# Wider and fewer zeros products in the early gaps of TensorE, in an attention-and-MLP kernel

## The chip, the cores and the metric

The kernel runs on one core of one Trainium2 chip. The metric is the device time of one execution in microseconds, as the median of several runs. A profile of one execution goes with it: its span is the time from the first instruction of the program to the last.

## The reference

Eight batches of an approximate attention (8 heads, 576 tokens, head size 64, 32 landmarks) are followed by a two-layer MLP with a squared ReLU. Cut to what matters:

```python
q_lm = q.reshape(B, H, m, S // m, D).mean(axis=3)      # 32 landmark means, k_lm alike
A  = softmax(scale * q    @ k_lm.T)
Bm = softmax(scale * q_lm @ k_lm.T)
C  = softmax(scale * q_lm @ k.T)
Z  = Bm.T / (norm_1(Bm) * norm_inf(Bm) + 1e-6)
for _ in range(6):
    Z = 2 * Z - Z @ Bm @ Z
x = (A @ Z @ C @ v), heads side by side                 # 4608 x 512
h = x @ w_in                                            # 512 -> 2048
out = square(max(h, 0)) @ w_out                         # 2048 -> 512
```

## The kernel before

**Staging.** The program is written as a list of operations (`attention(b)`, `mlp_in(b)`, `mlp_out(b)` for eight batches b). Each operation names what it reads and writes and is a small function that issues one or more instructions. The order in which they are issued is not that of the list: the table `ORDER` (lines 34 to 149) holds it, worked out beforehand. A positive code is an operation, an engine for it and a PSUM bank. A negative code is a fill: `emit` (lines 205 to 215) takes the bank from the code's last three bits and the count from the rest. Every engine then runs its own instructions strictly in that order, and semaphores hold an instruction until its data is there.

**The fills.** A fill multiplies a tile of zeros by itself into a PSUM bank that no other operation uses at that point (lines 392 to 394). Nothing reads the result. There are 15 groups of them, all in the first 34 us, where TensorE has gaps: in issue order 77, 11, 7, 10, 1, 7, 24, 4, 6, 4, 3, 10, 8, 3 and 3 products, 178 in all. Each is one load of weights (LDWEIGHTS, 128x128) and one product of 128 columns. The first group of 77 stands before any other work of TensorE; the tile `zero` that it reads is cleared by VectorE in `constants3` (line 399), the first of that function's clearings.

**The early stretch.** GpSimd issues the loads: k and q of batch 0, v, then k and q of batch 1, the four pieces of w_in and of w_out. All of these go through one queue. TensorE runs, for batch 0: transposes of k and q (line 519), landmark means (436), their fold (449), the small landmark scores (544), the scores C (677) and A (779), transposes of C (700), the first Newton product (600) and its six steps (632), C times v (728), the matrix W (763), and the transposes of A (835). Between these stand the first steps of batch 1: its transposes (519), means (473), fold (490), and landmark scores (541). Then line 850 folds w_in into G, line 870 is the first MLP layer and line 934 the second; from about 34 us on, these two make up most of TensorE's work. A transpose of four heads (line 519) is one operation of 12 products that all read the same loaded tile `kqraw` and the constant `ident`.

**Evacuation.** ScalarE and VectorE copy results out of PSUM (lines 267, 269, 273, 275), take maxima, sums and exponentials; GpSimd multiplies masks and normalises A.

## Time and profile before

| | us |
|---|---|
| median of 3 runs (263.9 to 264.46) | 264.15 |
| the profiled execution, its own time | 262.73 |
| its span | 261.0 |
| TensorE busy with products in the span | 251.1 |
| VectorE, ScalarE, GpSimd busy | 183.7, 179.4, 83.5 |

How to read what follows: PE is TensorE's products and PEld its weight loads, which overlap the products; DVE is VectorE, ACT is ScalarE, POOL is GpSimd, SP the engine that issues the stores. L394 is line 394 of the kernel. In a list in order of time a row gives the start, the length, the engine, the line, the operation and what it writes and reads; in brackets stands how long the engine was idle before it and what ended the idle time. "Issue" means that nothing in the profile ended it. A product's length runs from its start to a modelled end, and products overlap, so what a product costs is the distance from one start to the next. In rows by stretch of time, `(x96)` counts the instructions that ran in it. The TensorE clock is given as the share of full speed that was granted. Queues are named q0, q1, q8 and q14; the page calls q8 and q14 "instruction".

### The profile page before, as it was taken

What the parts mean: (1) busy time and instruction counts of PE and PEld (TensorE: products, weight loads), DVE (VectorE), ACT (ScalarE), POOL (GpSimd) and SP (SyncE); (2) the same over time, 40 slices, a digit from 0 to 9 for tenths busy, and PEclk for the clock granted to TensorE, in tenths of its full rate; (3) what the DMA queues carried; (4) which work ended last, traced back from release to release, by engine and by line L of the source; (5) the groups of instructions that cost most, each with busy time, mean ns of one, the idle gap of its engine ahead of it and who ended that gap; (6) DMA issues with size and microseconds to landing.
All of it is one profiled execution on the core that took longest, in us unless ns stands there. A gap on an engine that the chain in (4) does not pass through costs nothing.

```text
span 261.0 us, 7449 instructions
## 1 busy us (share of the span) xinstructions
PE 251.1 (96%) x3040; PEld 153.8 (59%) x3040; DVE 183.7 (70%) x423; ACT 179.4 (69%) x357; POOL 83.5 (32%) x127
## 2 busy tenths in 40 slices
PE   8996999999999999999999999999999999999992
PEld 8984674665555566556655565456655555555551
DVE  2395686779859998798668977866997676664400
ACT  1376789979973799786976697688787576454221
POOL 6153823526133525312471239124513220000000
PEclk9999689999999999999999999999999999999998
DMA  6999999694999999999969998999994107000425
GB/s 81 201 202 207 204 183 204 103 183 77 216 194 195 169 195 231 189 188 173 197 126 207 199 198 179 203 163 194 186 75 101 52 0 186 23 23 1 141 63 141
DMA packets 73346, 39.48 MB, mean 151 GB/s; under 512 B 46048, under 2 KB 68832, under 8 KB 73312
## 3 DMA queue, kind: packets, MB, share of 16 engines
q0 software_dynamic: 23040, 18.35, 46.9%
q1 hardware_dynamic: 50272, 20.65, 41.0%
q8 instruction: 24, 0.39, 0.6%
q14 instruction: 10, 0.08, 0.1%
HBM read 36.70 MB, written 9.44 MB: 177 GB/s over the span
## 4 chain that ended last, share of the span: by engine, by line
PE 83%; DMA 9%; issue 3%; DVE 1%; POOL 1%; ACT 1%; POOLq 0%; ACTq 0%; DVEq 0%
PE ps L934 45%; PE ps L870 22%; DMA kqraw<-in_k_dram 5%; DMA kqraw<-in_q_dram 4%; PE ps L850 3%; PE ps L779 2%; PE ps L473 2%; PE ps L728 1%; PE ps L394 1%; PE ps L637 1%; PE ps L519 1%; PE ps L677 1%; PE ps L700 1%; PE ps L490 1%; PE ps L835 1%
## 5 line engine op out<-in xcount | busy, mean ns | idle before, releaser
L934 PE MATMUL ps<-w_out_bf,gs 128*128 128x512 bf16 (+1 forms) x592 | 148.8, 374 | 0.0
L934 PEld LDWEIGHTS <-gs 128*128 128x128 bf16 x592 | 53.9, 98 | 44.0 <-issue 5.2
L870 PE MATMUL ps<-AT,G 128*128 128x288 bf16 x512 | 79.4, 287 | 0.1
L886 ACT ACTIVATE r<-ps 128x576 bf16<-128x576 f32 x84 | 53.5, 652 | 20.3 <-PE ps L870 14.2
L870 PEld LDWEIGHTS <-G 128*128 128x128 bf16 x512 | 49.2, 98 | 25.2 <-ACT G L267 0.5
L576 POOL TENSOR_TENSOR Pd<-st,ones_d 128x256 bf16<-128x256 bf16 x42 | 28.7, 683 | 81.6 <-DVE st L648 59.4
L895 ACT ACTIVATE gs<-r 128x576 bf16<-128x576 bf16 x70 | 45.5, 680 | 6.9 <-DVE r L888 6.5
L888 DVE TENSOR_SCALAR r<-ps 128x576 bf16<-128x576 f32 x44 | 32.7, 750 | 14.5 <-PE ps L870 10.6
L267 ACT CAST G<-ps 128x512 bf16<-128x512 f32 x47 | 25.6, 588 | 7.5 <-PE ps L850 7.1
L897 DVE TENSOR_TENSOR gs<-r 128x576 bf16<-128x576 bf16 x58 | 27.6, 490 | 4.1 <-ACT r L886 3.5
L814 POOL TENSOR_TENSOR EA<-EA,rA 96x384 bf16<-96x384 bf16 x20 | 18.3, 926 | 10.6 <-DVE st L648 6.2
L267 ACT COPY o<-ps 128x512 f32<-128x512 f32 (+1 forms) x19 | 10.8, 575 | 15.6 <-PE ps L934 14.6
L648 DVE SCALAR_TENSOR_TENSOR st<-st,ps 128x128 bf16<-128x128 bf16 x40 | 11.3, 282 | 13.8 <-PE ps L637 7.4
L269 DVE COPY o<-ps 128x512 f32<-128x512 f32 (+1 forms) x18 | 12.1, 669 | 10.3 <-PE ps L934 10.3
L788 DVE TENSOR_REDUCE mxA<-ps 96x16 f32<-96x512 f32 x24 | 16.1, 679 | 3.6 <-ACT gs L895 1.7
L394 PE MATMUL ps<-zero 128*128 128x128 bf16 x178 | 16.0, 256 | 1.1 <-DVE zero L399 1.1
L791 DVE TENSOR_TENSOR SA<-ps,mxA 96x512 f32<-96x512 f32 x24 | 16.2, 680 | 0.3
L803 DVE TENSOR_REDUCE sA<-EA 96x24 f32<-96x768 bf16 x16 | 15.0, 940 | 0.4 <-ACT EA L797 0.3
L797 ACT ACTIVATE EA<-SA 96x512 bf16<-96x512 f32 x24 | 14.5, 626 | 0.7 <-DVE SA L791 0.7
L394 PEld LDWEIGHTS <-zero 128*128 128x128 bf16 x178 | 13.6, 118 | 1.3 <-DVE zero L399 1.1
L269 DVE CAST G<-ps 128x512 bf16<-128x512 f32 x17 | 11.4, 684 | 3.0 <-PE ps L850 2.9
L688 ACT ACTIVATE EC<-ps,nmc 128x576 bf16<-128x576 f32 x16 | 11.9, 743 | 2.2 <-DVE nmc L683 2.1
(109 smaller groups left out, 246.4 us busy)
## 6 DMA issues: line engine op xcount, KB each, us to landing
kqraw<-in_k_dram POOLq DMA_DIRECT2D x8, 576.0 KB, 7.2
kqraw<-in_q_dram POOLq DMA_DIRECT2D x8, 576.0 KB, 11.6
vraw<-in_v_dram POOLq DMA_DIRECT2D x8, 576.0 KB, 9.1
out_dram<-o SPq DMA_DIRECT2D x23, 192.0 KB, 2.6
out_dram<-o SPq DMA_DIRECT2D x24, 128.0 KB, 2.6
w_in_bf<-in_moe_w_in_dram POOLq DMA_DIRECT2D x4, 512.0 KB, 10.0
w_out_bf<-in_moe_w_out_dram POOLq DMA_DIRECT2D x4, 512.0 KB, 11.3
out_dram<-o SPq DMA_DIRECT2D x23, 64.0 KB, 2.1
```

Of the source, the lines that this page charges most:

```text
L267: nc.scalar.copy(dst, src)
L269: ENG[e].tensor_copy(dst, src)
L394: mm(ps[:, bank, 0:P], lhsT=zero[:], rhs=zero[:], start=True, stop=True)
L576: ENG[e].tensor_tensor(dst[:], src.unsqueeze(2).to_broadcast([P, 2, NG, M]), ones_d[:].unsqueeze(1).to_broadcast([P, 2, NG, M]), ALU.mult)
L791: add({"DVE": dve(512)}, lambda e, sa=sa, j=j: nc.vector.tensor_tensor(grouped(SA[:, j, :]), grouped(one(sa)[0:TP, :]), mxA[:, j, :].unsqu ...
L814: ENG[e].tensor_tensor(w, w, rA[:, i, cs, :].rearrange("p c g -> p (c g)").unsqueeze(2) .to_broadcast([TP, NJ * NG, M]), ALU.mult)
L870: mm(t[:, j, 0:HALF], lhsT=G[:, i, f * P:(f + 1) * P], rhs=AT[:, i, j * HALF:(j + 1) * HALF], start=(i == 0), stop=(i == 1))
L886: nc.scalar.activation(rj, src, AF.Relu)
L888: nc.vector.tensor_scalar(out=rj, in0=src, scalar1=0.0, scalar2=None, op0=ALU.max)
L895: nc.scalar.activation(dst, r[:], AF.Square)
L897: nc.vector.tensor_tensor(dst, r[:], r[:], ALU.mult)
L934: mm(one(ok)[:, 0:hi - lo], lhsT=gs[:, f, x0:x0 + P], rhs=w_out_bf[:, f, lo:hi], start=(f == f0), stop=(f == f1 - 1))
```

## The change

A fill becomes a loop over up to eight units of 64 columns at a time: products of 512 columns and one narrower product for what is left. The tile of zeros grows from 128 to 512 columns, and the first 128 of them are the weights. The 15 fill codes of `ORDER` are rewritten: the count now stands for units of 64 columns. The banks and the places in the order are the same, and no other code is changed.

```diff
-    136, 24, 64, 104, 176, -616, 880, 802, 928, 404, 448, 856, -93, 480, 528, -61, 962, 1040, 1016, 224, 608, 4344,
+    136, 24, 64, 104, 176, -1280, 880, 802, 928, 404, 448, 856, -197, 480, 528, -117, 962, 1040, 1016, 224, 608, 4344,
...
-    zero = sb.tile([P, P], BF16, name="zero")
+    zero = sb.tile([P, 512], BF16, name="zero")
 
     def fill(bank, n):
-        for _ in range(n):
-            mm(ps[:, bank, 0:P], lhsT=zero[:], rhs=zero[:], start=True, stop=True)
+        while n:
+            w = min(n, 8)
+            mm(ps[:, bank, 0:64 * w], lhsT=zero[:, 0:P], rhs=zero[:, 0:64 * w], start=True, stop=True)
+            n -= w
```

Group by group, in issue order (products before, units of 64 columns after, products after):

| before | units | after |
|---|---|---|
| 77 | 160 | 20 |
| 11 | 24 | 3 |
| 7 | 14 | 2 |
| 10 | 20 | 3 |
| 1 | 3 | 1 |
| 7 | 14 | 2 |
| 24 | 50 | 7 |
| 4 | 8 | 1 |
| 6 | 12 | 2 |
| 4 | 9 | 2 |
| 3 | 6 | 1 |
| 10 | 20 | 3 |
| 8 | 18 | 3 |
| 3 | 6 | 1 |
| 3 | 6 | 1 |
| 178 | 370 | 52 |

## The prediction

> **What bounds the kernel now.** I read the page's busy times and chain first, then TensorE's waits, then the first 36 us in order of time, because every edited product stands there.

> ```profile
> PE 251.1 (96%) x3040; PEld 153.8 (59%) x3040; DVE 183.7 (70%) x423; ACT 179.4 (69%) x357; POOL 83.5 (32%) x127
> ...
> PE 83%; DMA 9%; issue 3%; DVE 1%; POOL 1%; ACT 1%; POOLq 0%; ACTq 0%; DVEq 0%
> ...
> q8 instruction: 24, 0.39, 0.6%
> ```
> ```profile
> PE ps L519 <- issue: 2.5, 1, 2.5
> ...
> PE ps L519 <- DMA kqraw<-in_k_dram: 0.5, 1, 0.5
> PE ps L473 <- DMA kqraw<-in_q_dram: 0.4, 1, 0.4
> ```

> TensorE is the bound: 83% of the chain is its own work. After its start it stands still only three times for 0.4 us or more, and the longest, 2.5 us, is put down to "issue": no semaphore that the profile shows released it. The stretches behind the start (length, PE busy, count of products started or running, granted clock, DMA share, GB/s) say what a shift is worth:

> ```profile
> 34.36:62.00 27.64, 27.64 (x329) 1.00 0.91 152
> 62.00:77.00 15.00, 14.35 (x176) 1.00 1.16 182
> 77.00:250.00 173.00, 172.84 (x1891) 1.00 0.83 145
> ```

> From 34.36 to 250 us TensorE lacks 0.65 + 0.16 = 0.81 us of being always busy. A microsecond lost or won before 34 us therefore passes nearly whole to the end, and the question is only what the early part does.

> **The fills themselves.** 15 groups hold 178 products of 128 columns; after the change they hold 52 of up to 512. Columns go from 178 x 128 = 22784 to 370 units x 64 = 23680, 896 more.

> ```profile
> 1.06 7.14 PEld L394 LDWEIGHTS <-zero 128*128 128x128 bf16 x77 [1.06 <-DVE zero L399]
> ...
> 15.15 1.36 PEld L394 LDWEIGHTS <-zero 128*128 128x128 bf16 x24
> 17.13 0.54 PEld L519 LDWEIGHTS <-kqraw 96*128 96x128 bf16 x12 [0.62 <-DMA kqraw<-in_k_dram]
> ```
> ```profile
> 39.02 0.86 PE ps L934 x4
> ```

> Warm, a fill of 128 costs 1.36 / 24 = 57 ns, and a product of 512 columns (line 934) 0.86 / 4 = 215 ns. The group of 24 becomes six of 512 and one of 128: 6 x 215 + 57 = 1.35 us against 1.36. So width buys nothing in stream time; columns decide. The 77 products at the start took 7.14 us, 93 ns each, more than the warm 57, and I let columns decide there too: the first group has 10240 in place of 9856, 4% or at most 0.3 us more. The zero tile grows from 128 to 512 columns, and its clearing goes ahead of the first fill:

> ```profile
> 0.90 0.11 DVE L399 MEMSET zero<- 128x64 uint32 x1 [0.90 <-PEq L987]
> 1.01 0.27 DVE L400 MEMSET kbd<- 128x256 uint32 x1
> ```

> The new clearing has the size of the one of kbd: 0.27 - 0.11 = 0.16 us later. Together up to 0.46 us, in front of the first transposes. What covers them is the wait of 0.45 us for batch 1's k at 17.13; its load stands in a queue of earlier loads that keeps the DMA busy (a share of 0.99 over the first 13.96 us, in a row further down), so its landing doesn't move. I take 0 for both; without the cover it is 0.46, and a gain has no source here.

> **The long idle, and what the fewer instructions do to it.** This is the term that counts. TensorE in order of time (start, length, what):

> ```profile
> 19.06 0.50 PE L394 MATMUL ps<-zero 128*128 128x128 bf16 x6
> 19.49 0.22 PE L600 MATMUL ps<-BTc 32*32 32x32 bf16 x8
> ...
> 22.03 0.56 PE L728 MATMUL ps<-vraw,ECT 96*32 96x64 bf16 x48
> 22.58 0.38 PE L490 MATMUL ps<-ident,lmk 128*128 128x128 bf16 x4
> 22.80 0.46 PE L519 MATMUL ps<-ident,kqraw 96*128 96x96 bf16 x7
> 25.78 0.39 PE L519 MATMUL ps<-ident,kqraw 96*128 96x96 bf16 x5 [2.52 <-issue]
> ```

> One operation of 12 transposes is cut after its seventh. No data can do that, since all 12 read the same two tiles. My reading: the instructions weren't there. The page's queue q8 carries 24 packets for 3040 products and 3040 weight loads, 253 instructions each as a floor; I take 256, or 128 pairs. Counts of products started by four times:

> ```profile
> 0.00:8.98 8.98, 7.92 (x96) 1.00 0.81 114
> 0.00:13.96 13.96, 12.90 (x223) 1.00 0.99 144
> 0.00:19.49 19.49, 17.97 (x329) 1.00 1.08 161
> 0.00:20.10 20.10, 18.58 (x351) 1.00 1.08 162
> 0.00:22.33 22.33, 20.81 (x460) 1.00 1.10 167
> 0.00:23.26 23.26, 21.74 (x479) 1.00 1.10 168
> ```

> The idle begins at pair 479. Going back by 128 gives 351 (20.10 us), 223 (13.96 us) and 95 (8.98 us). In the DMA view, the windows 8.98 to 11.51, 13.96 to 17.54 and 20.10 to 23.51 hold no packet of q8, and the windows that begin at 11.51, 17.54 and 23.51 hold one each. The last pair of windows:

> ```profile
> DMA packets 706, 0.71 MB, mean 207 GB/s; under 512 B 17, under 2 KB 706, under 8 KB 706
> q0 software_dynamic: 706, 0.71, 124.4%
> ...
> q8 instruction: 1, 0.02, 6.1%
> ```

> All 706 packets of 20.10 to 23.51 are q0's, the loads, which fill the DMA engines (124%). So a packet is asked for when a page of 128 pairs begins, starts 2.53, 3.58 and 3.41 us later behind the loads, and is needed when that page ends. At 20.10 the page lasted only to 23.10 (3.00 us), the packet began at 23.51, and TensorE went on at 25.77: a trip of 5.67, a loss of 5.67 - 3.00 = 2.67 us.

> Now the same count with fewer fills. By 19.49 nine groups have run, 147 products that become 41: 329 - 106 = 223, so that is where the page begins that begins at 13.96 now. By 22.33 eleven groups, 154 that become 44: 460 - 110 = 350, the next page. The page thus begins at 19.49 in place of 20.10 and lasts 22.33 - 19.49 = 2.84 us. With the same trip TensorE loses 5.67 - 2.84 = 2.83 us, inside the products of line 728: **+0.16 us**. The idle isn't removed; it moves some 0.8 us ahead. Its price from both sides: with the first packet's delay (2.53) the trip is 4.79 and the loss 1.95, or -0.72; with the second's (3.58) it is 5.84, or +0.33. I take the third's, whose traffic is the same.

> The page after that begins where 603 products have started now, less 124, which is 479:

> ```profile
> 0.00:32.63 32.63, 28.59 (x603) 0.92 1.14 179
> ```

> From 22.33 to 32.63, less the old idle of 2.67, are 7.6 us of work, longer than the trip, so no second idle. 126 pairs fewer are nearly one page of 128: later pages begin two pairs from where pages begin now. What lay under the old idle, the evacuations of lines 519 and 490 on ScalarE, partly comes after it instead; ScalarE stands idle then:

> ```profile
> 26.20 1.12 ACT L267 COPY kqT<-ps 128x1152 bf16<-128x1152 bf16 x1 [2.13 <-PE ps L519]
> ```

> Of its 2.13 us it gives up less than 1, so I cost this at 0; without that room, TensorE's next reader of kqT would wait the same up to 1 us.

> [...]

> **The clock behind the idle.** Pieces of half the cold period's length (granted clock in the third column from the right), and the two edges:

> ```profile
> 20.71:24.12 3.41, 2.55 (x102) 1.00 1.25 208
> 24.12:27.53 3.41, 1.75 (x44) 1.00 1.24 205
> 27.53:30.95 3.42, 3.42 (x63) 0.50 1.24 208
> 30.95:34.36 3.41, 3.41 (x47) 0.50 1.24 179
> ...
> 27.00:28.00 1.00, 1.00 (x30) 0.77 1.25 209
> 34.00:35.00 1.00, 1.00 (x8) 0.82 1.10 118
> ```

> After the idle the clock is halved from 27.53 to 34.36. What that costs:

> ```profile
> 17.83 0.40 PEld L700 LDWEIGHTS <-EC 128*96 128x96 bf16 x6
> ...
> 30.05 0.66 PEld L700 LDWEIGHTS <-EC 128*96 128x96 bf16 x6
> ```

> The same six transposes take 0.40 us warm and 0.66 cold, so a cold microsecond loses about 0.4. With the idle starting earlier, TensorE restarts at 19.49 + 5.67 = 25.16 rather than 25.77, and up to 0.6 us more of work may fall into the cold time: between 0 and 0.6 x 0.5 = **+0.3 us**. I take the upper end, since nothing ends the cold time earlier: the dense products that end it don't move.

> Sum: 0 + 0.16 + 0.3 = +0.46 us, about 0.5. The profiled execution (span 261.0, its own time 262.73) would be 263.2; the runs' median is 264.15, 1.4 above it, and becomes **264.6 us**.

> **Rivals.**
> - The clock falls one piece earlier. From 20.71 to 24.12 TensorE would be busy 22.33 - 20.71 = 1.62 us, less than the 1.75 that let the clock fall at 27.53. Then 25.16 to 27.53 is cold too: 2.37 x 0.4 = 0.95, with 0.16 together +1.1 (265.3); a piece more at the end adds 3.41 x 0.4 = 1.4 (266.7). Against it: the cut of the pieces may fall elsewhere in another execution. [...]
> - Packets come in a rhythm. They began at 11.51, 17.54 and 23.51, 6.0 us apart whatever was asked; then the next one stays at 23.51, TensorE restarts at 25.77 with 0.93 us more still to do, loses 3.44, and the sum is +0.8 to +1.1 (265.1).
> - Faster. The packet is asked for when the sequencer, not the array, reaches the page, and fewer instructions in front let it arrive earlier. With the first packet's trip of 4.79 the loss is 1.95: -0.7 (263.4). The point from which it decides is a packet that begins before 22.7, when the loss falls under 2.67. If an idle of 1.95 no longer halves the clock, 6.83 x 0.4 = 2.7 us go as well (260.7). For it: the first packet did come in 2.53. Against it: that was with the loads just begun.
> - Nothing changes: the idle belongs to that place for another reason and the fills are hidden: 264.15.

> **How the numbers follow.** A measurement tells 0.2%, 0.5 us, from no change. Forecast 0.40, by itself 264.1 to 265.0, so a little under half of it is beyond 0.2%; clock earlier or rhythm 0.25, all slower; faster 0.20; nothing 0.15. Slower is 0.18 + 0.25 = 0.43, same 0.21 + 0.15 = 0.36, faster 0.20 + 0.01 = 0.21. The range, 263.3 to 265.9, takes in the -0.7 of the shorter trip and both slower rivals without the extra cold piece; outside lie the two far clock cases.

> **What would show it.** TensorE idle by "issue" from about 22.4 to 25.2, inside line 728, and none at line 519; the q8 packet starting near 22.9; a packet at 23.5 and a restart at 25.8 would speak for the rhythm. The clock's low stretch beginning at 27.5 or at 24.1 decides between forecast and the first rival. Line 394 should show 52 products; 17.13 should still wait for k. The prediction is wrong if the idle vanishes, or if it stays at line 519.

## The result, and the profile after

| | before | changed |
|---|---|---|
| median of 20 runs each, in turn, us | 263.96 (261.39 to 265.26) | 261.16 (258.97 to 265.64) |
| the profiled execution: its time, its span, us | 262.73, 261.0 | 258.97, 257.3 |
| granted clock over the span | 0.984 | 1.000 |

The ratio is 0.9878, with a 95% interval of 0.9848 to 0.9908: the change makes the kernel **1.2% faster**. The ratios leave out executions more than 1.5% above the fastest of their kernel (five of the changed kernel's 20; with all of them in, the quotient of the two medians is 0.9894), and four of the profiled executions below, whose times are given with them, are such ones.

The page of the changed kernel: engines, the instruction queue, the chain of waits.

```profile
PE 248.2 (96%) x2914; PEld 143.9 (56%) x2914; DVE 183.7 (71%) x423; ACT 179.1 (70%) x357; POOL 83.3 (32%) x127
...
q8 instruction: 23, 0.38, 0.5%
...
PE 77%; DMA 10%; DVE 4%; issue 3%; POOL 2%; ACT 2%; POOLq 0%; DVEq 0%; ACTq 0%
```

TensorE has 126 products fewer (2914 against 3040), and q8 carries 23 packets in place of 24: one page of instructions less. TensorE is still the bound. Its waits in the changed kernel (line, what it waited for, us in total, times, longest):

```profile
PE ps L395 <- DVE zero L401: 1.3, 1, 1.3
PE ps L730 <- issue: 1.2, 1, 1.2
```

The long idle put down to "issue" was 2.5 us at line 519. It is now 1.2 us at line 730, which is line 728 of the kernel before. In order of time (start, length, what, and in brackets the idle time ahead of it):

```profile
1.26 6.38 PE L395 MATMUL ps<-zero 128*128 128x512 bf16 x20 [1.26 <-DVE zero L401]
...
16.92 0.69 PE L521 MATMUL ps<-ident,kqraw 96*128 96x96 bf16 x12 [0.72 <-DMA kqraw<-in_k_dram]
...
19.27 0.22 PE L602 MATMUL ps<-BTc 32*32 32x32 bf16 x8
...
21.77 0.50 PE L730 MATMUL ps<-vraw,ECT 96*32 96x64 bf16 x41
23.46 0.24 PE L730 MATMUL ps<-vraw,ECT 96*32 96x64 bf16 x7 [1.19 <-issue]
...
24.47 0.24 PE L634 MATMUL ps<-st 32*32 32x64 bf16 x8
...
30.12 2.64 PE L872 MATMUL ps<-AT,G 128*128 128x288 bf16 x20
```

One operation of 48 products is cut after its 41st. The counts of products started say which one it is (stretch, length, TensorE busy and count, clock, DMA share, GB/s), and the same view in shorter stretches shows the clock:

```profile
0.00:19.26 19.26, 17.28 (x223) 1.00 1.08 163
0.00:22.27 22.27, 20.29 (x351) 1.00 1.10 169
...
27.53:30.95 3.42, 3.36 (x63) 1.00 1.23 204
30.95:34.36 3.41, 3.41 (x26) 1.00 1.24 207
30.67:62.00 31.33, 31.18 (x375) 1.00 1.05 169
62.00:77.00 15.00, 14.72 (x162) 1.00 1.24 197
77.00:246.00 169.00, 168.52 (x1847) 1.00 0.82 144
```

TensorE stops at pair 351, and the page of 128 pairs that it has then used up began with pair 223, at 19.26 us. The clock, halved from 27.53 to 34.36 before, stays at 1.00. The packet of the missing page, from the DMA view of 19.26 to 21.18 and of 21.18 to 22.20 (packets, MB, share of the DMA engines):

```profile
q0 software_dynamic: 399, 0.39, 123.6%
...
q0 software_dynamic: 199, 0.20, 118.7%
q8 instruction: 1, 0.02, 5.7%
```

It began at 21.18, 1.92 us after its page began (3.41 before), and TensorE restarted at 23.46: a trip of 23.46 - 19.26 = 4.20 us where it had been 5.67. From the packet to the restart it is 23.46 - 21.18 = 2.28 us, and it was 25.77 - 23.51 = 2.26: the whole difference lies ahead of the packet.

**The accounting.** Two operations of the kernel before serve as marks, a Newton step and the first product of the first MLP layer:

```profile
26.10 0.24 PE L632 MATMUL ps<-st 32*32 32x64 bf16 x8
...
33.79 2.90 PE L870 MATMUL ps<-AT,G 128*128 128x288 bf16 x20
```

The Newton step comes 1.63 us earlier (24.47 against 26.10): 2.52 - 1.19 = 1.33 of it is idle time saved, and the other 0.3 is an earlier start of the stretch. From there to the first MLP layer the same work (but for 128 columns more of fills) takes 30.12 - 24.47 = 5.65 us in place of 33.79 - 26.10 = 7.69: 2.04 us, which I put down to the clock. Together 3.67, of the 3.76 that separate the two profiled executions. From 30.67 to 246 TensorE lacks only 0.15 + 0.28 + 0.48 = 0.91 us of being always busy, so the lead lasts in this execution.

The medians lie 2.80 apart, less than the 3.76. Of the 20 executions of the changed kernel that enter a ratio (15 here, 5 in a repetition), 13 had a granted clock of 0.995 or more and a median of 259.71; 7 had less than 0.99 and a median of 261.64. So the clock's 1.9 us were won in 13 of the 20. No execution of the kernel before, beside any of the experiments, was above 0.992.

### The profile page after: what moved, and what is told of

Its sections match the earlier page's. It is cut to its first block, busy times and chain, and to the rows that moved or that the text cites. A ratio compares the mean times of both kernels' runs of the same rounds, so it can differ in the third digit from the quotient of the medians.

```text
span 257.3 us, 7197 instructions
## 1 busy us (share of the span) xinstructions
PE 248.2 (96%) x2914; PEld 143.9 (56%) x2914; DVE 183.7 (71%) x423; ACT 179.1 (70%) x357; POOL 83.3 (32%) x127
## 4 chain that ended last, share of the span: by engine, by line
PE 77%; DMA 10%; DVE 4%; issue 3%; POOL 2%; ACT 2%; POOLq 0%; DVEq 0%; ACTq 0%
PE ps L936 43%; PE ps L872 21%; DMA kqraw<-in_k_dram 5%; DMA kqraw<-in_q_dram 5%; PE ps L852 3%; PE ps L475 2%; PE ps L781 2%; PE ps L730 1%; PE ps L639 1%; PE ps L521 1%; PE ps L395 1%; POOL EA L816 1%; ACT EC L690 1%; POOL Pd L578 1%; PE ps L492 1%
## 5 line engine op out<-in xcount | busy, mean ns | idle before, releaser
L872 PEld LDWEIGHTS <-G 128*128 128x128 bf16 x512 | 49.0, 98 | 25.2 <-issue 0.7
L267 ACT CAST G<-ps 128x512 bf16<-128x512 f32 x47 | 25.7, 590 | 6.5 <-PE ps L852 6.0
L267 ACT COPY o<-ps 128x512 f32<-128x512 f32 (+1 forms) x19 | 10.8, 576 | 15.6 <-PE ps L936 15.5
L816 POOL TENSOR_TENSOR EA<-EA,rA 96x384 bf16<-96x384 bf16 x20 | 17.6, 890 | 8.8 <-DVE st L650 6.4
L395 PE MATMUL ps<-zero 128*128 128x512 bf16 (+5 forms) x52 | 14.3, 400 | 1.3 <-DVE zero L401 1.3
L685 DVE TENSOR_REDUCE nmc<-ps 128x1 f32<-128x576 f32 x16 | 11.8, 749 | 1.0 <-PE ps L679 1.0
```

The source lines that it names most:

```text
L267: nc.scalar.copy(dst, src)
L395: mm(ps[:, bank, 0:64 * w], lhsT=zero[:, 0:P], rhs=zero[:, 0:64 * w], start=True, stop=True)
L816: ENG[e].tensor_tensor(w, w, rA[:, i, cs, :].rearrange("p c g -> p (c g)").unsqueeze(2) .to_broadcast([TP, NJ * NG, M]), ALU.mult)
L872: mm(t[:, j, 0:HALF], lhsT=G[:, i, f * P:(f + 1) * P], rhs=AT[:, i, j * HALF:(j + 1) * HALF], start=(i == 0), stop=(i == 1))
```

## The experiments

The questions: is it the width of the fills or the place of the pages that counts; why is the trip shorter; and does the early lead stay. "Pairs" are a product with its weight load. Unless said otherwise an experiment starts from the changed kernel, and its `fill` gets a special case for the first group (160 units), in which narrower products give the same columns in more instructions:

```diff
     def fill(bank, n):
+        if n == 160:
+            for _ in range(48):
+                mm(ps[:, bank, 0:64], lhsT=zero[:, 0:P], rhs=zero[:, 0:64], start=True, stop=True)
+            n -= 48
         while n:
```

### Pairs put back: 42, 112, 84

The diff above adds 42 pairs (48 products of 64 columns and 14 of 512 in place of 20).

> The wide kernel with 42 more pairs of weight load and product (the first group: 48 products of 64 columns and 14 of 512 in place of 20 of 512; the same columns, the same zeros). Page theory (an idle time arises where 128 pairs run faster than the next packet of instructions comes): the pages then begin near 14.6, 20.4 and 25.5 us, each long enough or nearly so; TensorE's idle by issue shrinks from 1.2 us to 0 to 1.0 us and moves to line 519's or 632's place near 25; 259.3 to 260.8 us, at or under the wide kernel's 261.2. Width theory (fewer, wider products are the gain by themselves, by fewer weight loads or a steadier clock): a third of the removed pairs is back, so the time is no better than the wide kernel's, 261.2 to 262.2.

Measured: 263.49 us, ratio 0.9984 (0.9936 to 1.0031). TensorE in order of time, and VectorE:

```profile
27.38 0.19 PE L638 MATMUL ps<-st 32*32 32x32 bf16 x2 [1.02 <-issue]
```
```profile
138.90 0.69 DVE L269 COPY o<-ps 128x512 f32<-128x512 f32 x1 [3.01 <-DMA out_dram<-o]
```
```profile
PE ps L940 <- DVE o L269: 2.1, 1, 2.1
...
PE ps L734 <- ACT o L267: 1.0, 1, 1.0
```

The early part is as good as the change's (idle of 1.02, clock at 1.00, a lead of 33.79 - 30.33 = 3.46 us on the kernel before when the first MLP layer starts), but the time is above the expected range. At 85 us TensorE waits 1.0 us for ScalarE's copy of an output, which had waited 1.31 us for a store; at 139 us VectorE waits 3.01 us for a store to free the output tile, and TensorE 2.1 us for VectorE. Behind that 0.1 us of the lead is left. VectorE's wait is in the profile neither of the kernel before nor of the changed one.

With `range(128)` and `n -= 128`, 112 pairs are added, and the count of instructions is nearly that of before.

> The wide kernel with 112 more pairs (the first group: 128 products of 64 columns and 4 of 512; the same columns), so that the pages begin where they begin in the kernel before, while the other 14 groups stay wide. Page theory: the idle is back in the transposes of batch 1 near 22.5 to 23.2 us with 1.5 to 2.8 us, and the time is the kernel's before, 263 to 264.3. Width theory: 14 of 15 groups are wide as in the changed kernel and the columns are the same, so 261 to 262.

Measured: 263.87 us, ratio 0.9974 (0.9919 to 1.0028). TensorE in order of time, and the clock:

```profile
25.60 0.47 PE L525 MATMUL ps<-ident,kqraw 96*128 96x96 bf16 x7 [1.71 <-issue]
```
```profile
26.65:33.48 6.83, 6.50 (x104) 0.50 1.23 201
```

The idle is back in the transposes, the clock falls for 6.83 us, and the time is that of before, though 14 of the 15 groups are still wide. So width by itself isn't the gain: with the pages' edges nearly where they were, the gain is gone.

With `range(96)` and `n -= 96`, 84 pairs are added.

> The wide kernel with 84 more pairs (the first group: 96 products of 64 columns and 8 of 512; the same columns). Page theory: the worst place, with an idle near 24.1 of 0.3 to 1.8 us and a second one near 51.4 of 0.7 to 2.2 us; 262 to 265, slower than the wide kernel by 1 to 3. Width theory: as the wide kernel, 261 to 262.

Measured: 266.44 us, ratio 1.0105 (1.0052 to 1.0158). TensorE, its clock, and VectorE:

```profile
26.03 0.31 PE L683 MATMUL ps<-kqT,qdup 64*32 64x288 bf16 x6 [1.49 <-issue]
```
```profile
28.00:29.00 1.00, 1.00 (x17) 0.77 1.23 204
31.00:32.00 1.00, 1.00 (x18) 0.52 1.25 204
```
```profile
141.68 0.69 DVE L269 COPY o<-ps 128x512 f32<-128x512 f32 x1 [3.34 <-DMA out_dram<-o]
```

An idle of 1.49, the clock halved for a shorter time, and again the store at 142 us. The expected second idle near 51 us didn't come, and yet the time is above the expected range. The first MLP layer starts at 31.98, still 1.81 us ahead of the kernel before: what makes this kernel the slower one comes later.

### More instructions instead of fewer

From the kernel before: 56 of the first 77 fills are split in two of 64 columns each, so 56 pairs are added to it.

```diff
     def fill(bank, n):
+        if n == 77:
+            for _ in range(112):
+                mm(ps[:, bank, 0:64], lhsT=zero[:], rhs=zero[:, 0:64], start=True, stop=True)
+            n -= 56
         for _ in range(n):
```

> The kernel before with even narrower products: of the first 77, 56 are split into two of 64 columns, 56 pairs more than before, no wide product anywhere. Page theory: pages move by 56 pairs the other way and begin near 19.9 and 25 us, so the idle shrinks to 0 to 1.5 us, near 25; 260 to 262 us, faster than before by 2 to 4. Width theory: more and narrower products can't be faster; 264 or slower.

Measured: 269.08 us, ratio 1.0170 (1.0115 to 1.0226). TensorE in order of time, and the counts up to its restarts:

```profile
24.59 0.53 PE L732 MATMUL ps<-vraw,ECT 96*32 96x64 bf16 x45 [1.31 <-issue]
...
30.51 0.23 PE L636 MATMUL ps<-st 32*32 32x32 bf16 x5 [1.96 <-issue]
```
```profile
0.00:24.50 24.50, 20.79 (x479) 1.00 1.09 166
0.00:30.45 30.45, 24.61 (x607) 1.00 1.12 174
```

The expectation missed: two idles, at pairs 479 and 607, instead of a short one, and slower instead of faster. The place is right (479 + 128 = 607). The page that begins at the restart of 24.59 is the one to look at: its successor lets TensorE go on at 30.51, a trip of 5.92 us. In the kernel before, too, the packet behind such a restart came late, 29.49 - 25.77 = 3.72 us after it. In this profiled execution, of 271.38 us, the first MLP layer starts at 34.80, 1.0 us later than before; more is lost behind that, in waits of 2.5 us for a load of q and of 1.9 us for VectorE's copy of an output.

### The change again, and fewer loads

The changed kernel without an edit.

> The changed kernel again, to see whether its idle and clock repeat. Page theory: the idle lies again in line 730 near 22 us with 0.9 to 2.0 us, the clock stays up in about half of the executions, 260.2 to 262.2 us. If the first profile was luck alone: an idle of 2.5 us or more and 263 or more.

Measured: 260.51 us, ratio 0.9841 (0.9793 to 0.9888). The idle is again in line 730 and as long:

```profile
23.98 0.24 PE L730 MATMUL ps<-vraw,ECT 96*32 96x64 bf16 x7 [1.18 <-issue]
```

This profiled execution took 265.27 us. It had a lead of 33.79 - 30.64 = 3.15 us at the first MLP layer and lost it between 95 and 116 us: in a wait of 1.7 us for a load of q, a halved clock for 3.41 us, and a wait of 1.7 us for ScalarE's copy of an output, which had waited 2.5 us for a store.

From the kernel before: three pieces of `w_in` and one of `w_out` are not loaded; GpSimd fills them with 0.03, so the outputs are not the reference's.

```diff
         def load_wi(e):
+            if j < 3:
+                nc.gpsimd.memset(w_in_bf[:, :, j * 512:(j + 1) * 512], 0.03)
+                return
...
         def load_wo(e):
+            if j == 0:
+                nc.gpsimd.memset(w_out_bf[:, 0:4, :], 0.03)
+                return
```

> The kernel before, but the first three pieces of w_in and the first of w_out are written by GpSimd as a constant and not loaded, so that the load queue is empty from about 20.3 us on; the outputs are not the reference's. Theory that the packet of instructions waits behind the loads: it comes within 1 us of the page's beginning near 20.1, the 2.5 us of idle in line 519 are gone, the clock stays up, and TensorE's first MLP product (33.8 before) starts near 29 to 31. Theory that the idle has another cause, or that fetching a page takes its time without loads too: an idle of 2 us or more stays at line 519.

Measured: 261.46 us, ratio 0.9893 (0.9841 to 0.9945). TensorE, then the DMA view of 20.68 (where pair 351 stands) to 22.05 and of 22.05 to 23.05:

```profile
24.40 0.39 PE L525 MATMUL ps<-ident,kqraw 96*128 96x96 bf16 x5 [0.60 <-issue]
```
```profile
q0 software_dynamic: 262, 0.26, 114.7%
...
q0 software_dynamic: 29, 0.02, 13.5%
q8 instruction: 1, 0.02, 6.1%
```

The fills and their count are those of before, and so is the place, but the idle is 0.60 in place of 2.52 and the clock stays at 1.00. The packet began just as the loads ran dry (114.7%, then 13.5%). So the idle is a wait for a packet of instructions behind the loads. This is the most direct evidence for it. The packet came 1.37 us after its page began, not within the 1 us that was expected.

### Half of the change

Only the first group wide (19 products of 512 and one of 128; 57 pairs fewer than before). `ORDER` has the fill codes of the kernel before, and `fill` is:

```diff
     def fill(bank, n):
+        if n != 77:
+            for _ in range(n):
+                mm(ps[:, bank, 0:P], lhsT=zero[:, 0:P], rhs=zero[:, 0:P], start=True, stop=True)
+            return
+        n *= 2
         while n:
```

> One part alone: only the first group is wide (20 products for 77, the same columns), all others as before; 57 pairs fewer. Page theory: pages begin near 16.4, 21.4 and 24.5 us; an idle of 0 to 1.0 near 21.4 and a second of 1.2 to 2.8 near 24.5, so hardly any gain: 262.5 to 265.5. Width theory: the first group has 43% of the columns and 45% of the pairs removed, so about half of the gain: 262 to 263.

Measured: 269.85 us, ratio 1.0136 (1.0081 to 1.0192). TensorE in order of time, the counts, and the third idle among the waits:

```profile
22.40 0.34 PE L526 MATMUL ps<-ident,kqraw 96*128 96x96 bf16 x4 [0.43 <-issue]
...
28.32 0.20 PE L548 MATMUL ps<-kbd,qdup 64*32 64x32 bf16 x4 [2.18 <-issue]
```
```profile
0.00:22.38 22.38, 19.59 (x351) 1.00 1.09 168
0.00:28.30 28.30, 23.33 (x479) 1.00 1.13 176
0.00:58.50 58.50, 52.05 (x863) 0.97 1.09 175
```
```profile
PE ps L941 <- issue: 1.5, 1, 1.5
```

Half of the change is slower than none, and slower than expected. The idles stand at pairs 351, 479 and 863 (each is 128 times a whole number, less 33, as are the 479 of the kernel before, the 351 of the changed one and the 479 and 607 of the narrower one), and the second trip is 28.32 - 22.40 = 5.92 us, after a stall as in the narrower kernel. The early idles alone don't make it slower: its first MLP layer starts at 33.16, 0.6 us ahead of the kernel before, and the rest is lost in the third idle and in later waits.

The other half: the condition is `n == 77`, so the first group stays at 77 products of 128 columns and the other 14 are wide (72 pairs fewer than before).

> The other part alone: the first group as before, the other 14 wide with the same columns as before; 72 pairs fewer, 55 of them before 22.3 us. Page theory: the pages begin near 16.6, 21.4 and 24.5 as with the first part alone, so the same two idles and hardly any gain, 262.5 to 265.5; the two parts' gains don't add up to the whole's. Width theory: half of the gain, 262 to 263.

Measured: 264.83 us, ratio 0.9995 (0.9945 to 1.0044). TensorE in order of time and its waits:

```profile
26.34 0.38 PE L786 MATMUL ps<-kbd,kqT 128*128 128x64 bf16 x7 [0.83 <-issue]
...
29.57 1.63 PE L877 MATMUL ps<-AT,G 128*128 128x288 bf16 x12
```
```profile
PE ps L480 <- DMA kqraw<-in_q_dram: 2.5, 1, 2.5
PE ps L941 <- DVE o L269: 2.4, 1, 2.4
```

The first MLP layer starts at 29.57, 4.2 us ahead of before and the earliest of all. One idle came where two were expected. In this profiled execution, of 267.38 us, all of the lead is gone at 140 us, after a wait for a load of q (at 74 us) and the store's wait. The early part is not the whole story.

### A few pairs around the change

Four pairs more: the special case makes 8 products of 256 columns (`n -= 32`) ahead of 16 of 512.

> The wide kernel with 4 pairs more (the first group: 8 products of 256 columns and 16 of 512; the same columns). The third page then begins 4 pairs earlier, ahead of the wait for BTc at the first landmark product. Read-ahead theory (the packet is asked for when the sequencer reads up to the page, and a waiting instruction in front of the page holds it back): nothing is held back, the idle stays at 0.7 to 1.2 us near 22; 260 to 261.3 us. Place theory (a trip of 4.2 us from the page's beginning): the same here; this is the control of the next run.

Measured: 259.73 us, ratio 0.9837 (0.9796 to 0.9878), with one idle of 0.98 at the same place: as the changed kernel.

Four pairs fewer: the first group has 16 products of 512 (2048 columns fewer), and the page begins inside the products of line 602.

```diff
-    136, 24, 64, 104, 176, -1280, 880, 802, 928, 404, 448, 856, -197, 480, 528, -117, 962, 1040, 1016, 224, 608, 4344,
+    136, 24, 64, 104, 176, -1024, 880, 802, 928, 404, 448, 856, -197, 480, 528, -117, 962, 1040, 1016, 224, 608, 4344,
```

> The wide kernel with 4 pairs fewer (the first group: 16 products of 512 columns in place of 20, 2048 columns fewer, ahead of the landing of k that TensorE waits for anyway). The third page begins 4 pairs later, behind the wait for BTc. Read-ahead theory: the sequencer can't pass that wait before 19.1, the packet is asked for 1 us or more later than in the wide kernel, the idle near 22 grows from 1.2 to 2.0 to 3.0 us and the clock falls in most executions: 262 to 264.5 us. Place theory: 4 pairs change the page's length by 0.1 us; idle 1.1 to 1.4, 260 to 261.5.

Measured: 262.98 us, ratio 0.9927 (0.9888 to 0.9966). TensorE in order of time, and its clock:

```profile
25.05 0.24 PE L730 MATMUL ps<-vraw,ECT 96*32 96x64 bf16 x3 [1.98 <-issue]
```
```profile
24.57:34.81 10.24, 9.10 (x133) 0.50 1.18 189
```

The profiled execution took 264.66 us; a granted clock below 0.99 was found in six of the eight executions that enter the ratio, too. The idle is 1.98 instead of 1.19, and the packet began at 22.66, 2.60 us after its page began at 20.06 (1.92 in the changed kernel). The page begins 0.80 later here too, which follows a later landing of batch 1's k. The read-ahead theory of the expectation fits this pair: in the changed kernel the page begins in front of line 602, which reads VectorE's `BTc`; with four pairs fewer it begins behind. But the request for a page isn't in the trace, so the theory isn't shown, and the packet is only 0.7 us later here, counted from its page, which is less than expected.

Fourteen pairs more (`range(16)`, `n -= 16`) and 28 more (`range(32)`, `n -= 32`):

> The wide kernel with 14 pairs more (16 products of 64 columns and 18 of 512 first; the same columns). Place theory: the page begins 0.6 us earlier and ends 0.1 us earlier, so the idle shrinks to 0.4 to 0.8 us; read-ahead theory: the packet was already asked for as early as the queue lets it, so the idle stays near 0.9 to 1.3. Either way the later pages move by 14 pairs only; 259.3 to 261.3 us, at best 1 us under the wide kernel.

> The wide kernel with 28 pairs more (32 products of 64 columns and 16 of 512 first; the same columns). Place theory: no idle or up to 0.5 us near 21.9; read-ahead theory 0.3 to 1.2 us. The lead at the first MLP product is as the wide kernel's or up to 1 us better. Later pages move by 28 pairs; if that brings the waits for stores and loads of the kernel with 42 more, 262 to 264, otherwise 259 to 261.

Measured: 262.73 us, ratio 0.9891 (0.9825 to 0.9957), idle 0.62, and 260.28 us, ratio 0.9863 (0.9818 to 0.9908). TensorE in order of time in the second:

```profile
23.19 0.45 PE L734 MATMUL ps<-vraw,ECT 96*32 96x64 bf16 x35 [0.90 <-issue]
...
29.11 0.48 PE L706 MATMUL ps<-ident,EC 128*96 128x128 bf16 x5 [1.10 <-issue]
```

The idle of 0.62 with 14 more is in the range of the place theory (0.4 to 0.8) and below the read-ahead theory's (0.9 to 1.3). The first idle of 0.90 with 28 more is in the read-ahead theory's range (0.3 to 1.2) and above the other's (none to 0.5). So neither theory foretells both. With 28 more there are two shorter idles, 29.11 - 23.19 = 5.92 us apart once more. From the changed count to 28 pairs above it, all four kernels gain about alike: their intervals overlap, and none is shown to beat the change.

### Is the late loss one of place?

In four of the kernels so far VectorE waits for the store (42 and 84 put back, the narrower one, and the other groups wide). Their later pages lie 42 to 56 pairs away from the nearest page of the kernel before; those of all others lie within 30, but for the one with only the first group wide, which lies 57 away and has no such wait. Two edits test whether that decides. First the changed kernel with 42 second-layer products of batch 0 split in two of 256 columns, which moves the later pages and leaves the early part alone:

```diff
+                            if f0 < f < f1 - 1 and b == 0 and 2 * t + hp < 7:
+                                for c0 in (0, 256):
+                                    mm(one(ok)[:, c0:c0 + 256], lhsT=gs[:, f, x0:x0 + P],
+                                       rhs=w_out_bf[:, f, c0:c0 + 256], start=False, stop=(f == f1 - 1))
+                                return
```

> The changed kernel, early part untouched, with 42 pairs more between 36 and 60 us: 42 products of the second MLP layer of batch 0 are split into two halves of 256 columns. Late-page theory (the kernels with 42 to 84 pairs more lost their lead after 75 us because their later pages begin elsewhere): the lead at the first MLP product is the wide kernel's (near 30.1 to 30.7 us), and 1.5 to 4 us of it are lost later, with a wait for a store near 140: 262 to 264.5. Rival (those losses come from the early part's timing or from chance): 260 to 261.5, no such wait.

Measured: two executions of 260.2 us and four of 264.8 to 271.8, a median of 265.37; the ratio of 0.9843 (0.9799 to 0.9887) rests on the two alone. The wait of TensorE for VectorE:

```profile
PE ps L941 <- DVE o L269: 1.1, 1, 1.1
```

The wait appears, shorter than elsewhere (VectorE waits 1.96 us for the store), in a profiled execution of 260.22 us. This run is inconclusive.

Second, the kernel with 42 pairs put back, whose lead was lost, with 86 products split late (all of batch 0's inner ones and some of batch 1's), so that its later pages begin where they do in the changed kernel (42 + 86 = 128), two pairs from those of the kernel before:

```diff
+                            if f0 < f < f1 - 1 and (b == 0 or (b == 1 and (0 < t < 3 or (t == 3 and f < 11)))):
```

> The kernel with 42 pairs more early, and 86 more between 36 and 75 us in the same way, so that the later pages begin where they begin in the changed kernel (42 + 86 = 128). Late-page theory: the lead of 3 us and more at the first MLP product is kept, no wait for a store near 140: 259.8 to 261.8. Rival: 263 to 264.5 as with the 42 alone.

Measured: 260.73 us, ratio 0.9857 (0.9826 to 0.9889), against 263.49 and 0.9984 without the split. The early idle is 0.79, and TensorE waits for no output tile (ScalarE waits 1.49 us for a store at 84 us). With 86 pairs more it is 1% faster, as the theory of place foretold. That is one pair of kernels. It supports the theory, but doesn't show it: the kernel with only the first group wide doesn't fit, the first edit left it open, and in the profile of the change's repetition the lead was lost with no page moved. How a page's place would make a store late was not found.

### All of them together

| kernel | early pairs against the change | idles at a page's end, us | clock then halved | ratio to before | profiled execution, us |
|---|---|---|---|---|---|
| before | +126 | 2.52 | yes | 1 | 262.73 |
| before, more instructions | +182 | 1.31, 1.96 | after the second | 1.0170 | 271.38 |
| before, fewer loads | +126 | 0.60 | no | 0.9893 | 260.25 |
| 112 put back | +112 | 1.71 | yes | 0.9974 | 263.12 |
| 84 put back | +84 | 1.49 | yes | 1.0105 | 266.12 |
| first group wide | +69 | 0.43, 2.18, 1.52 | after the second alone | 1.0136 | 267.46 |
| the others wide | +54 | 0.83 | no | 0.9995 | 267.38 |
| 42 put back | +42 | 1.02 | no | 0.9984 | 263.60 |
| the same, pages moved back | +42 | 0.79 | no | 0.9857 | 260.71 |
| 28 more | +28 | 0.90, 1.10 | no | 0.9863 | 259.09 |
| 14 more | +14 | 0.62 | no | 0.9891 | 259.47 |
| 4 more | +4 | 0.98 | no | 0.9837 | 259.68 |
| the change | 0 | 1.19 | no | 0.9878 | 258.97 |
| the change again | 0 | 1.18 | no | 0.9841 | 265.27 |
| the change, later pages moved | 0 | 1.20 | no | 0.9843 | 260.22 |
| 4 fewer | -4 | 1.98 | yes | 0.9927 | 264.66 |

The idles and the clock are those of the one profiled execution of each kernel, whose time is in the last column.

## Why the prediction was wrong

**What held.** TensorE is the bound, and a microsecond won before 34 us came through to the end, in the changed kernel's profile. The idle is a wait for a page of 128 pairs (the two stops of the narrower kernel, at pairs 479 and 607, lie just so far apart); it moved from line 519 into line 728, to pair 351, as counted. It is preceded by a page that began at 19.26 (predicted 19.49). There are 52 products at line 395, the wait for k still covers the fills (16.92), and no second idle came.

**The step that failed** is "I take the third's, whose traffic is the same": a delay of 3.41 us from a page's beginning to the packet of the next one, a trip of 5.67 us, and so a loss of 2.83. The delay measured 1.92, the trip 4.20 and the loss 1.19, a term of 1.19 - 2.52 = -1.33 instead of +0.16. The traffic was indeed the same (123.6% and 118.7% of the DMA engines against 124.4%); it doesn't fix the delay. Nor was the trip of 4.20 luck: the other two profiles with the change's early part have 4.18 and 4.20. With the loads running, a DMA share near 1.25, and the page counted back 128 products from the idle, the trip was about 4.5 us with four pairs more, 4.9 with 112 put back, 5.0 with the others wide, 5.1 with 42 put back, 5.6 with 84 put back and 6.0 in the narrower kernel; with four fewer it was 25.05 - 20.06 = 4.99. From the packet to the restart it was 2.26 to 2.39 us wherever the packet's start was read (before, the change, four fewer, fewer loads). As far as the traces show it, then, it is the delay that differs, with the place of the page's edge among the instructions.

Why it does was not shown. After a stop for instructions the delay was 3.72 us in the kernel before (25.77 to 29.49) and 3.65 in the changed one (23.46 to 27.11), and three of the trips after one measured 5.92. But a page with no such stop ahead of it had 3.58 (13.96 to 17.54 in the kernel before), and the trip of 6.0 in the narrower kernel had none ahead either, so the stops aren't the whole of it. The lower bound taken for the loss, 1.95 from a trip of 4.79, was not low enough either.

**The clock term** had the wrong sign. "+0.3" came from a cold time that begins earlier; it fell away altogether, which was worth -2.04 between the marks. That dense products end the cold time, as the prediction took it, no run shows: in the kernel before TensorE was busy for all of 27.53 to 30.95, and the clock stayed halved to 34.36. The wrong sign followed from the first error: the piece of 3.41 us that holds the idle of 1.19 has TensorE busy for 2.22 us, where the kernel before had 1.75 and the clock fell; an idle of 2.83 would have left as little as 0.58, if it lay in one piece. The prediction's bounds for the fetch (-0.72 and +0.33) were not carried through to the clock, so the range ended at 263.3, above the result.

**The rival that came true** is "Faster", by its point of decision: a packet before 22.7, which began at 21.18. Its reason, an earlier request, was not shown, since no trace has the request, and fewer instructions in front are not enough for a short delay: with four pairs fewer than the change the packet came 2.60 us after its page, not 1.92. Its 260.7 with the clock kept is near the 261.16 of the median, partly by luck: it took a loss of 1.95 where 1.19 was measured, and the clock was kept in 13 of 20 executions, not in all. The rival got a chance of 0.20 because the only short delay (2.53) was put down to loads that had just begun. The other rivals are out: no rhythm of 6.0 us (the packet was not at 23.5), no clock piece earlier, and the idle was not fixed to line 519.

**A size that was off without harm:** "columns decide" for the first group. It took from 1.26 to 7.58 us, 6.32 for 10240 columns, where 9856 in narrow products took 8.21 - 1.06 = 7.15, so width did save stream time there; the wait for k hid it. The 0.2 us later start (1.26 against 1.06) is the wider clearing (0.27 us in place of 0.11), predicted as 0.16.

**The other packets.** The packet of 21.18 began inside the page of 19.26 to 22.27. Of the kernel before's 24 packets and the changed kernel's 23, one each left TensorE a long idle, 2.52 and 1.19 us; in the other kernels the table has one to three such idles, of 0.43 to 2.18 us.

## What to carry to other kernels

When TensorE stands still inside one operation and nothing released it, count its products: here the stops lay 128 pairs apart, or a multiple of it, and TensorE went on 2.26 to 2.39 us after a packet of q8 began. Fewer loads at that time shortened the stop here from 2.52 to 0.60 us, another place of the page's edge to 1.19. The delay of a packet, counted from its page's beginning, can't be carried over from one page to another because the traffic is alike: here it was 1.9 to 3.7 us at a DMA share of 1.24 to 1.33. Take bounds as wide as that, and carry them on to the clock. A change in the number of instructions moves every later page too, so look at the whole trace before crediting an early gain: here leads of 3.5 and 4.2 us were lost between 74 and 140 us.
